# The second transform with 128 + 65 contraction rows for all four kinds

## The chip, the core and the metric

The kernel runs on one core of one Trainium2 chip. The metric is the device time of one launch in microseconds (us), all four batches included. A core has a matrix engine (PE, with its weight loads listed as PEld), three elementwise engines (DVE, ACT, POOL), and DMA queues; each engine takes its own instructions in a fixed order, and semaphores tie the engines together.

## The reference

There are 4 batches of 768 tokens with 8 heads of 48 channels (384 in all). What is computed, cut to what matters:

```python
for t in range(S):                       # complex linear recurrence with decay a (normalized)
    S_re, S_im = ar*S_re - ai*S_im + kv, ar*S_im + ai*S_re
    y[:, :, t] = einsum('bhd,bhde->bhe', q[:, :, t], S_re)
x = y                                    # as (batch, 768, 384)
u = x + real(fft(fft(x, axis=1), axis=2))
un = (u - mean) / sqrt(var + 1e-6)
v = u + relu(un @ w_ch1) @ w_ch2
u2 = v + token_mlp(v)                    # 768 -> 256 -> 768 over the tokens
out = u2 + relu(u2 @ w3) @ w4
```

## The kernel before

**Two streams.** A batch passes through a chain (`stage1`: the recurrence, a scan on DVE, ACT and POOL, then attention-like matmuls in chunks of 96 tokens; `stage2`: the two-axis transform and the normalization) and then through a dense stream (`mlp`, `tok1`, `tok2`: matmuls of 128 x 384 in three passes each, lines 989 and 1011 above all). The chain of batch b+1 is written next to the dense stream of batch b, so PE has dense matmuls to run while the chain waits. Batch 0 has no dense stream beside its chain: there, conversions of the weights (ACT, DVE, POOL) and warming matmuls (`warm`, L320) run in the gaps. After the chain of batch 3 only dense work is left.

**Order.** The source gives each instruction a priority by stream (`RANK`, `Prio`), and the order of every engine's queue is made when the program is built: a list scheduler walks a simulated timeline and gives an engine that comes free the ready instruction of best priority. On the chip each queue then runs in that fixed order. A tile framework adds the semaphores: it tracks which columns of a tile an instruction reads and writes.

**stage2.** All of its data lie in one 128 x 12288 tile, the one that holds the two halves K and Q of stage 1 (the trace calls it `qkt`). `WSP` (L1019) gives each part its columns; the folded columns `fd` lie at 3072 to 6160, over K of chunks 4 to 7, and K of chunk 7 is read last by the score matmuls of that chunk (L809).

1. `folds` (L1040) adds and subtracts the two halves of the 768 tokens (L1047, L1053), as the output of stage 1 (`xT`) comes in.
2. `mirrors` (L1059) folds columns n and 384 - n into `fd` (L1063; the unpaired columns 0 and 192 by ACT copies, L1070). There are four kinds `ty`: cosine or sine for odd or even sums. They fill 192, 192, 193 and 191 of the 193 columns: `kinds` (L1038), where a sine kind is shifted by one column.
3. `dft` (L1073), called with `kt` 1 and 0, transforms the channels: for each kind four matmuls (L1079) whose stationary operand is `fd[:, ty, r, dt, n0:n0+n]`, 112 rows by n columns, and whose moving operand is 97 columns of cosines or sines. `n` comes from `ZK` (L1021): 128 for `kt` 0; for `kt` 1 it is 64, 64, 65 and 63. ACT copies the n result rows to `Z` (L1081).
4. `smm` (L1101) transforms the tokens: for one kind, two matmuls (L1104) add up over 128 rows and then `ZK[ty][1]` rows; the stationary operand is `smat` (constants, zero behind the last row of each kind), the moving one 193 columns of `Z`. There are eight calls per batch, in three groups `i`: kinds 0, 1; then 0, 2, 1, 3; then 2, 3, with four small matmuls for one extra row (L1109) ahead of the last one of kind 3. After each group ACT copies the result (L1140), POOL adds and subtracts its halves (L1141, L1142), PE transposes `xT` (L1151), and DVE joins both into `u` (L1156); statistics and `un` follow (L1163 to L1185), and `transposed` (L969) hands `un` to the dense stream.

All matmuls here are in 32-bit floats, and the trace lists each as two weight loads and two matmul records.

Of the kernel before, what the change touches and what calls it, by code (L numbers as in the profile page):

```python
# [53 lines left out]
def attn_fft_mixer_kernel(ctx: ExitStack, tc: tile.TileContext, aL, xL, vL, wL, qN, kN, vN, arN, aiN,  # L54
# [18 lines left out]
    ve, se, ge = Prio(nc.vector, "v"), Prio(nc.scalar, "v"), Prio(nc.gpsimd, "v")  # L73
# [28 lines left out]
    def palloc(tag, shape):  # L102
        n = 1
        for s in shape[1:]:
            n *= s
        if tag == "s":
            turn3[0] += 1
            tag = ("ssc", "s", "sp")[lent[0]]
            tag = tag[turn3[0] % len(tag)]
        t = psum.tile([128, 512], F32, tag=tag, bufs=PSB[tag], name=tag)  # L110
        v = t[0:shape[0], 0:n]
        if len(shape) == 3:
            v = v.rearrange("p (a b) -> p a b", b=shape[2])
        return v
# [861 lines left out]
    def mlp(u, b, p0, th, tl, done):  # L976
        for qd in range(4):
# [40 lines left out]

    WSP = {"xd": (0, 3072), "fd": (3072, 3088), "xf": (6160, 3072), "Z": (6160, 1552), "xr": (7712, 1536),  # L1019
           "smat": (9248, 2048), "cb": (0, 1737), "cc": (1737, 1158), "un": (3072, 2304)}  # L1020
    ZK = ((128, 64), (128, 64), (128, 65), (128, 63))  # L1021

    def stage2(b, space):
        def part(name, pat=None, **kw):
            o, n = WSP[name]
            v = space[:, o:o + n]
            return v.rearrange(pat, **kw) if pat else v
# [7 lines left out]
        xd = [[xd[:, s, r] for r in range(2)] for s in range(2)]  # L1035
        fd = part("fd", "p (t r a b) -> p t r a b", t=4, r=2, a=2)[0:112]
        Z = part("Z", "p (a b) -> p a b", a=8)
        kinds = ((0, 0, ALU.subtract, 0, 191), (1, 0, ALU.add, 1, 192), (2, 1, ALU.add, 0, 192), (3, 1, ALU.subtract, 1, 191))  # L1038

        def folds(k, o, n):  # L1040
# [32 lines left out]
        def dft(kt):  # L1073
            for ty in range(4):
                n0, n = 128 * kt, ZK[ty][kt]
                ps = palloc("s", [128, 2, 97])
                for r in range(2):
                    for dt in range(2):
                        te.matmul(out=ps[0:n, r, :], lhsT=fd[:, ty, r, dt, n0:n0 + n], rhs=dcos[0:112, ty % 2, dt, r, :],  # L1079
                                  start=(dt == 0), stop=(dt == 1))  # L1080
                se.copy(out=Z[0:n, 2 * ty + kt, :].rearrange("p (i r) -> p r i", r=2), in_=ps[0:n])  # L1081

# [18 lines left out]
        def smm(o, ty, j0, first, last, extra=False):  # L1101
            for kt in range(2):
                kk = ZK[ty][kt]
                te.matmul(out=o, lhsT=smat[0:kk, ty, kt, j0:j0 + 128], rhs=Z[0:kk, 2 * ty + kt, 0:193],  # L1104
                          start=(first and kt == 0), stop=(last and kt == 1))
                if extra and kt == 0:
                    for k2 in range(2):
                        kk = ZK[2][k2]
                        te.matmul(out=o[0:1], lhsT=fk[0:kk, k2:k2 + 1], rhs=Z[0:kk, 4 + k2, 0:193], start=False, stop=False)  # L1109

# [159 lines left out]
    def chain(b):  # L1270
        return stage2(b, stage1(b))
# [29 lines left out]
    with tc.If(fv != 0):  # L1301
        with tc.For_i(0, B, 1) as b:
            fallback(b)
            u, norm = stage2(B, alloc("qk", [128, 12288], name="ws"))
            t = transposed(u, norm, "s")
            dense2(B, u, *dense1(B, u, *t), row=b)
# [111 lines left out]
```

## Time and profile before

| what | us |
|---|---|
| median of 3 runs | 1066.04 |
| lowest and highest run | 1060.92, 1067.02 |
| the profiled execution, its own time | 1067.39 |
| its span in the profile | 1065.6 |

The span runs from the first to the last instruction of the program; some 1.8 us of the execution's time lie around it. Busy times are of that one execution. The ends of matmul records are modelled, so what a matmul costs is read from the distance between starts. A weight load can run under the matmul before it, so an idle stretch ahead of a weight load is time in which the engine had not let it begin.

### The profile page before, as it was taken

The numbers are of one execution on the slowest core, as the hardware profiler recorded it, in microseconds if no ns is written. First come the engines' busy times: TensorE is split into PE (matmuls) and PEld (weight loads), VectorE is DVE, ScalarE is ACT, GpSimd is POOL, SyncE is SP. The second block draws the span as 40 slices with busy tenths as digits, with TensorE's granted clock in tenths as the row PEclk, the third lists the DMA queues.
The fourth block names the chain that finished last, engine by engine and source line by source line (L and its number), as shares of the span: only waits on it lengthen the run. The fifth ranks groups of instructions, "written<-read, shape, count | busy, mean of one in ns | idle before, by whom it ended". The sixth has DMA issues, their size and how long they took to land.

```text
span 1065.6 us, 21108 instructions
## 1 busy us (share of the span) xinstructions
PE 976.5 (92%) x7326; PEld 916.8 (86%) x7326; DVE 750.0 (70%) x2078; ACT 507.5 (48%) x1423; POOL 393.3 (37%) x544
## 2 busy tenths in 40 slices
PE   1459896999889989999999999999999999999997
PEld 0238775999889878999998899999889999999997
DVE  6986867999998696999768979984844433433332
ACT  6752546877775335678413766842233212111211
POOL 5632765555464782346336412424622002000000
PEclk9986987999999889999999999999999999999999
DMA  6226953678657942666575346655315434543522
GB/s 222 53 80 166 315 202 130 219 233 265 231 166 223 241 143 88 211 188 195 163 181 163 107 142 191 185 156 169 98 46 163 133 115 144 163 137 128 172 93 77
DMA packets 98337, 173.09 MB, mean 162 GB/s; under 512 B 10928, under 2 KB 57904, under 8 KB 97712
## 3 DMA queue, kind: packets, MB, share of 16 engines
q1 hardware_dynamic: 98224, 171.67, 52.4%
q8 instruction: 60, 0.98, 0.4%
q14 instruction: 53, 0.43, 0.1%
HBM read 132.31 MB, written 39.32 MB: 161 GB/s over the span
## 4 chain that ended last, share of the span: by engine, by line
PE 61%; DVE 2%; POOL 1%; DMA 1%; issue 1%; ACT 1%; SPq 0%; POOLq 0%; ACTq 0%
PE l L1011 22%; PE l L989 22%; PE s L809 2%; PE s L685 1%; PE s L1079 1%; PE s L1104 1%; PE s L1218 1%; PE s L1236 1%; DVE qkt L1053 1%; PE s L864 1%; PE c L1104 1%; PE c L685 1%; PE l L1236 1%; DMA cvt<-wL 1%; PE s L1151 1%
## 5 line engine op out<-in xcount | busy, mean ns | idle before, releaser
L1011 PE MATMUL l<-w,h 128*128 128x384 f32 x1728 | 325.8, 339 | 1.1 <-DVE h L1002 1.0
L989 PE MATMUL l<-th,w 128*128 128x384 f32 x1152 | 313.9, 341 | 4.1 <-ACT th L972 2.2
L1011 PEld LDWEIGHTS l<-w,h 128*128 128x128 f32 x1728 | 298.1, 188 | 4.5 <-DVE h L1002 2.1
L989 PEld LDWEIGHTS l<-th,w 128*128 128x128 f32 x1152 | 209.9, 189 | 6.4 <-ACT th L972 3.0
L993 ACT ACTIVATE h<-l 128x384 fp32r<-128x384 f32 x192 | 94.1, 491 | 211.4 <-PE l L989 211.1
L989 PE MATMUL l<-tl,w 128*128 128x384 f32 x576 | 194.3, 337 | 0.0
L1014 DVE TENSOR_TENSOR u<-u,l 128x384 f32<-128x384 f32 x192 | 105.4, 549 | 77.0 <-PE l L1011 75.9
L1002 DVE SCALAR_TENSOR_TENSOR h<-l,h 128x384 fp32r<-128x384 f32 x160 | 88.4, 553 | 88.7 <-ACT h L993 87.8
L989 PEld LDWEIGHTS l<-tl,w 128*128 128x128 f32 x576 | 108.9, 189 | 0.2
L207 POOL TENSOR_TENSOR cvt<-cvt 128x384 int32<-128x384 int32 x56 | 58.9, 1056 | 28.3 <-DVE cvt L205 22.9
L217 POOL TENSOR_TENSOR w<-cvt,w 128x384 fp32r<-128x384 f32 x44 | 46.0, 1050 | 52.2 <-ACT w L216 45.1
L1203 POOL TENSOR_TENSOR xl<-u,xh 128x384 fp32r<-128x384 f32 x18 | 18.1, 1015 | 98.0 <-ACT xh L1202 98.0
L499 PE MATMUL s<-misc,y 128*112 128x128 f32 x64 | 14.9, 378 | 42.1 <-DMA fk<-cFk 19.5
L203 ACT ACTIVATE cvt<-cvt 128x384 int32<-128x384 uint32 x56 | 31.3, 559 | 44.0 <-DMA cvt<-wL 41.2
L499 PEld LDWEIGHTS s<-misc,y 128*112 128x112 f32 x64 | 9.6, 181 | 47.9 <-POOL ss L463 22.8
L634 POOL TENSOR_TENSOR A<-raw,tm 128x144 f32<-128x144 f32 (+1 forms) x51 | 25.4, 499 | 61.9 <-DVE tm L632 24.7
L1000 POOL TENSOR_TENSOR h<-full,h 128x384 fp32r<-128x384 f32 x32 | 33.0, 1030 | 39.0 <-ACT full L999 37.2
L658 DVE TENSOR_TENSOR p<-p,A 128x144 f32<-128x144 f32 x144 | 44.6, 310 | 1.6
L616 POOL TENSOR_TENSOR tm<-tm 128x144 f32<-128x144 f32 (+1 forms) x51 | 25.3, 498 | 45.3 <-ACT tm L615 43.0
L660 DVE TENSOR_TENSOR p<-p,yt 128x96 f32<-128x96 f32 x144 | 37.5, 260 | 2.2
L809 PE MATMUL s<-qkt 112*96 112x96 f32 x328 | 38.6, 267 | 0.0
L845 POOL TENSOR_TENSOR yc<-Aa,gm 48x384 f32<-48x384 f32 x18 | 19.8, 1101 | 48.1 <-DVE Aa L835 47.7
(310 smaller groups left out, 2023.4 us busy)
## 6 DMA issues: line engine op xcount, KB each, us to landing
w<-wscr SPq DMA_DIRECT2D x180, 384.0 KB, 3.6
cvt<-wL SPq DMA_DIRECT2D x56, 384.0 KB, 4.6
wscr<-w SPq DMA_DIRECT2D x44, 384.0 KB, 3.0
Kn<-kn SPq DMA_DIRECT2D x56, 192.0 KB, 4.2
kn<-y SPq DMA_DIRECT2D x96, 96.0 KB, 2.6
raw<-aL SPq DMA_DIRECT2D x48, 144.0 KB, 3.4
xx<-xL SPq DMA_DIRECT2D x48, 144.0 KB, 3.3
V<-vL SPq DMA_DIRECT2D x32, 144.0 KB, 3.2
```

Source lines behind the costliest of these rows:

```text
L203: se.activation(out=lo, in_=lo.bitcast(U32), func=ACTF.Copy, scale=2.0 ** -29)
L207: x = ge.tensor_tensor(out=a, in0=a, in1=lo, op=ALU.add)
L217: ge.tensor_tensor(out=parts[:, 1, :], in0=a.bitcast(F32), in1=r32(parts[:, 0, :]), op=ALU.subtract)
L658: ve.tensor_tensor(out=cur, in0=prev, in1=A[:, j, 0:3, :], op=ALU.mult)
L660: ve.tensor_tensor(out=cur[:, 0:2, :], in0=cur[:, 0:2, :], in1=y, op=ALU.add)
L809: te.matmul(out=ps[:, j, :], lhsT=K[:, hc, :], rhs=Q[:, hc, :])
L989: te.matmul(out=ps, lhsT=w1[:, wi, kt * 128:kt * 128 + 128], rhs=x[g][:, kt, :], start=(n == 0), stop=(n == 8))
L993: x = se.activation(out=hi, in_=ps, func=ACTF.Relu)
L1000: ge.tensor_tensor(out=lo, in0=full, in1=r32(hi), op=ALU.subtract)
L1002: ve.scalar_tensor_tensor(out=lo, in0=ps, scalar=0.0, in1=r32(hi), op0=ALU.max, op1=ALU.subtract)
L1011: te.matmul(out=ps, lhsT=hs[m][:, hi, tt * 128:tt * 128 + 128], rhs=w2[:, wi, :], start=(n == 0), stop=(n == 8))
L1014: ve.tensor_tensor(out=u[tt], in0=u[tt], in1=ps, op=ALU.add)
```

## The change

The contraction of `kt` 1 gets 65 rows for every kind, where it had 64, 64, 65 and 63: `dft(1)` loads 65 columns of `fd` as weights and makes 65 rows of `Z`, and the second matmul of each `smm` contracts 65 rows. So that the added columns hold zeros, `stage2` first sets columns 191 and 192 of all 16 rows of `fd` to zero, by one DVE instruction per call; the mirrors and copies of the kinds that use those columns write them afterwards. `smat` needs no change. The number of matmuls, their moving columns and the DMAs stay as they are.

```diff
@@ -1018,7 +1018,7 @@
-    ZK = ((128, 64), (128, 64), (128, 65), (128, 63))
+    ZK = ((128, 65),) * 4
@@ -1035,6 +1035,7 @@
         fd = part("fd", "p (t r a b) -> p t r a b", t=4, r=2, a=2)[0:112]
         Z = part("Z", "p (a b) -> p a b", a=8)
+        ve.memset(fd[:, :, :, :, 191:193], 0.0)
         kinds = ((0, 0, ALU.subtract, 0, 191), (1, 0, ALU.add, 1, 192), (2, 1, ALU.add, 0, 192), (3, 1, ALU.subtract, 1, 191))
```

## Rows read from the trace of the kernel before

**Rows 1.** The page: the span, and PE's busy time, share and instructions.
```profile
span 1065.6 us, 21108 instructions
PE 976.5 (92%) x7326; PEld 916.8 (86%) x7326; DVE 750.0 (70%) x2078; ACT 507.5 (48%) x1423; POOL 393.3 (37%) x544
```

**Rows 2.** The page: the chain that ended last, shares of the span.
```profile
PE 61%; DVE 2%; POOL 1%; DMA 1%; issue 1%; ACT 1%; SPq 0%; POOLq 0%; ACTq 0%
```

**Rows 3.** Windows in stage 2: stretch, length, busy us of PE, PEld, DVE, ACT, POOL, clock.
```profile
155.70:166.50 10.80, 10.23 (x56) 6.95 (x55) 5.95 (x18) 4.33 (x11) 9.03 (x13) 1.00 0.37 146
...
389.50:395.20 5.70, 5.65 (x29) 5.25 (x29) 5.67 (x13) 3.00 (x12) 5.70 (x7) 0.50 0.18 51
...
579.00:609.00 30.00, 29.58 (x190) 25.52 (x189) 27.21 (x96) 19.76 (x65) 16.44 (x29) 1.00 0.51 155
764.00:792.00 28.00, 28.00 (x182) 24.05 (x181) 14.06 (x44) 11.16 (x28) 9.60 (x12) 1.00 0.22 71
```

**Rows 4.** Waits of PE between 575 and 800 us: total, times, longest.
```profile
PE s L864 <- issue: 1.3, 1, 1.3
...
PE c L1079 <- POOL qkt L1063: 0.4, 1, 0.4
```

**Rows 5.** Timeline of PE, batch 2: start us, duration us, group of records.
```profile
598.88 3.76 PE L1104 MATMUL c<-qkt 128*128 128x193 f32 x16
...
606.54 1.15 PE L1104 MATMUL c<-qkt 128*128 128x193 f32 x6
```

**Rows 6.** Timeline of PEld, the same stretch; in brackets the idle time before.
```profile
599.30 0.29 PEld L1104 LDWEIGHTS c<-qkt 64*128 64x128 f32 x2 [0.23 <-issue]
599.82 0.96 PEld L1104 LDWEIGHTS c<-qkt 128*128 128x128 f32 x6 [0.23 <-issue]
601.00 0.29 PEld L1104 LDWEIGHTS c<-qkt 64*128 64x128 f32 x2 [0.23 <-issue]
```

**Rows 7.** Groups of L1104 by shape, 580 to 615 us: count | busy, mean ns.
```profile
L1104 PE MATMUL c<-qkt 64*128 64x193 f32 x8 | 2.4, 375 | 0.0
...
L1104 PE MATMUL c<-qkt 65*128 65x193 f32 x4 | 1.0, 327 | 0.0
```

**Rows 8.** All of L1104: idle time of PEld before it, us, times.
```profile
  issue: 8.4, 35
```

**Rows 9.** Timeline of PE, batch 3: the channel transform.
```profile
764.86 0.88 PE L1079 MATMUL s<-dcos,qkt 112*64 112x97 f32 x8
765.58 0.83 PE L1079 MATMUL c<-dcos,qkt 112*64 112x97 f32 x8
766.34 0.88 PE L1079 MATMUL s<-dcos,qkt 112*65 112x97 f32 x8
```

**Rows 10.** Groups by shape, 760 to 800 us: weight loads of the channel transform.
```profile
L1079 PEld LDWEIGHTS s<-dcos,qkt 112*65 112x65 f32 x8 | 0.7, 136 | 0.1
...
L1079 PEld LDWEIGHTS s<-dcos,qkt 112*63 112x63 f32 x8 | 0.7, 135 | 0.2 <-ACT qkt L1081 0.2
```

**Rows 11.** Timeline of ACT, end of batch 0's stage 2.
```profile
165.82 0.48 ACT L1140 COPY qkt<-s 128x386 f32<-128x386 f32 x1 [2.10 <-PE s L1104]
166.20 0.21 ACT L1173 ACTIVATE rs<-rs 128x2 f32<-128x2 f32 x1
```

**Rows 12.** Timeline of PE, the same part: the first transposes to the dense stream.
```profile
171.20 1.11 PE L969 MATMUL s<-misc,qkt 128*128 128x128 f32 x4 [3.63 <-DVE qkt L1185]
```

**Rows 13.** Groups of DVE by shape: memsets of the kernel before.
```profile
L420 DVE MEMSET p<- 64x48 f32 x2 | 0.2, 98 | 0.8 <-PEq L1408 0.8
...
L128 DVE MEMSET ones<- 128x1 f32 x1 | 0.1, 59 | 0.0
```

**Rows 14.** Timeline of DVE, batch 2: the first fold.
```profile
567.72 0.96 DVE L1047 TENSOR_TENSOR qkt<-xT 112x768 f32<-112x768 f32 x1 [0.83 <-ACT xT L872]
```

**Rows 15.** Timeline of PE, batch 2: the scores of chunk 7.
```profile
569.04 0.84 PE L809 MATMUL s<-qkt 112*96 112x96 f32 x8
```

**Rows 16.** Timeline of PE, batch 1: the first group of the channel transform.
```profile
389.55 0.88 PE L1079 MATMUL p<-dcos,qkt 112*64 112x97 f32 x4 [2.19 <-DVE qkt L1063]
```

## The prediction

> **What bounds the kernel now.** I read the page first. PE is busy for 976.5 of 1065.6 us [rows 1], and the chain that ended last lies on PE for 61% of the span, on no other engine for more than 2% [rows 2]. So time taken from PE should count, if it is taken where PE has nothing to wait for. Next I read windows around the four calls of `stage2` [rows 3]. In batches 2 and 3 PE is full (29.58 of 30.00 us, 28.00 of 28.00), since dense matmuls fill what the transform leaves; between 575 and 800 us its longest wait is 1.3 us, and one wait of 0.4 us belongs to the transform [rows 4]. Batch 1 has one dry spell: PE waits 2.19 us for a mirror on DVE [rows 16], and then runs for 5.70 us at a granted clock of 0.50, the lower of its two levels (1.2 instead of 2.4 GHz) [rows 3]. In batch 0 nothing dense is at hand, and PE is busy for 10.23 of 10.80 us in the token transform [rows 3].
>
> Then I read the matmuls that change. A "busy" PE can hide a loss, so I read starts, not durations. In the timeline of weight loads an idle stretch of 0.23 us stands ahead of each load of 64 rows, and the same ahead of the first 128-row load behind it [rows 6]. The releaser is given as "issue": nothing that the profile knows was late. Inside the group of six loads at 599.82 (128, 65, then 128 rows of kinds 0, 2, 1) no idle time is listed: from 128 to 65 rows PE goes on. So it is the step between over 64 rows and at most 64 that costs. The means agree: a matmul record of 64 rows takes 375 ns, one of 65 rows 327 [rows 7]. Over the kernel these stops come 35 times ahead of L1104, 8.4 us of idle loader in all [rows 8]; the stops that follow a small matmul and stand ahead of another line come on top.
>
> **Part 1: the token transform.** Of the eight `smm` of a batch six end in 64 or 63 rows. The last of them comes behind the one-column matmuls of L1109, and the step from one weight column stays a step. So a batch loses 5 steps in and 6 out, 11; four batches lose 44. The price of one: 16 records without dense work between span 3.76 us and hold 5 steps [rows 5]. A record's own length at the end is 0.33 [rows 7], so 15 distances take 3.43. Six records with no step span 1.15, so 5 distances take 0.82, or 0.165 each [rows 5]. 15 x 0.165 is 2.48, the excess 0.95, and a step costs 0.19 us. It is less than the idle 0.23 because a load otherwise starts under the matmul before. All of PE: 44 x 0.19 = 8.4 us.
>
> Batches 1 to 3: 33 x 0.19 = 6.3 us, counted whole, because PE is full there. Batch 0: 11 x 0.19 = 2.1 us. There ACT waits 2.10 us for the last `smm` group, and a rescaling step, L1173, is queued right behind that copy [rows 11]; the norm of the first tokens needs it, and PE idles 3.63 us for the norm [rows 12]. So an earlier end of `smm` passes through ACT to the dense stream. DVE's chain behind it sets part of this end and may keep some: 0 to 2.1, I take 1.5.
>
> **Part 2: the channel transform.** It has the step in the number of weight columns. In batch 3 two groups of eight 64-column records start 0.72 us apart, while the 65-column group starts 0.76 behind the second [rows 9]. Counting from the second group's start to its end 0.83, the next starts 0.07 before that end; the second started 0.16 before the first one's (764.86 + 0.88). That is 0.09 lost at the step, and the group behind a step is 0.05 longer (0.88 against 0.83): 0.14 us each. In batches 1 to 3 I count nine such steps that stand beside no longer wait: two or three a batch where dense work or another kind comes between, 1.3 us; those beside a wait, and batch 0's, I count at nothing (upper end: six more, 0.8). The added column costs nothing that can be seen: a load of 65 columns takes 136 ns, one of 63 takes 135 [rows 10]. The ACT copies of 65 rows have as many columns as those of 63.
>
> **Part 3: the memset.** It writes 32 elements in 112 rows. The nearest rows are 59 ns for 1 element and 98 for 48 [rows 13]; I take 0.09 us, 0.4 in all. It lies on DVE, which in batches 1 to 3 is not what PE waits for but at the dry spell; I count it at 0 (upper end 0.4). Its wait matters more. `fd` lies over K of chunk 7, so the memset waits for the scores of chunk 7, which the mirrors did before; but in the source it stands ahead of the folds. If it is also queued ahead of them, folds and the dense stream's DVE work behind it wait. In batch 2 the first fold starts at 567.72 [rows 14], the scores end at 569.04 + 0.84 = 569.88 [rows 15]: at most 2.2 us of DVE, before mirrors that start later anyway. POOL's and ACT's writes to `fd` already wait for DVE's folds, so they gain no later wait. I take 0 because the list scheduler gives the queue to what is ready first; the upper end is 4 x 2.2 = 8.8.
>
> **Sum.** 6.3 + 1.5 + 1.3 = 9.1 us. Against the profiled execution: 1067.4 - 9.1 = 1058.3. That execution lies 1.35 us above the median, so from the median it is 1056.9. I forecast 1057.5, between them. All steps at full price and no cost give 8.4 + 2.1 = 10.5, which is 1056.9 or, from the median, 1055.5.
>
> **Rivals.**
> 1. *The memset stalls the folds* in each batch (8.8 us): 1067.4 - 9.1 + 8.8 = 1067, no change. For it: its place in the source. Against: folds and memset have one stream's priority, and only the ready one is taken.
> 2. *PE runs dry ahead of the channel transform in more batches*, the other side. The queues are ordered anew when the program is built, with one more DVE instruction per batch; where the folds come behind more dense additions on DVE, PE has no matmul left. For it: it happens in batch 1. Against: nothing in the change asks for it. Price from batch 1: 2.19 us idle, and half of 5.70 us at the lower clock, 2.85: 5.0 each. From two more spells on, it eats the gain; three give 1067.4 - 9.1 + 15.0 = 1073.3.
> 3. *The new order takes batch 1's dry spell away*: 1058.3 - 5.0 = 1053.3. Nothing speaks for it but that the queues are made anew.
> 4. *PE's time is not what counts*: the steps go, and PE waits as much longer for the chain. Then batch 0's 1.5 us are left: 1066. Against it stand the full windows [rows 3].
> 5. *It does not do what it says*: a 65-row load stops PE as well. The group at 599.82 speaks against it [rows 6]. Then the time stays at 1067. The Trainium skill ("TensorE: Matmul & The Clock Gate", Part 3, the mechanism) has a rule that would lead there: weight loads overlap running matmuls only where their row groups differ, and 65 rows share theirs with the 128 before. By that rule the gain is nothing and the time 1067; the trace disagrees, for the loads at 599.82 run on without idle time.
>
> **How the numbers follow.** Forecast 0.58 (its own range 1054.5 to 1061, from the bounds of parts 1 to 3 and the two baselines); rivals 1 to 5: 0.10, 0.09, 0.10, 0.08, 0.05. The range 1052 to 1067 holds the forecast, rivals 3 and 4 and about half of rivals 1 and 5. About 1% is what a measurement of this kernel can tell from no change: 10.7 us, just over the most that the steps can give. Faster by over 1% is rival 3 and a part of the forecast's lower end: 0.25. Slower by over 1% is the worse half of rival 2: 0.05. Within 1%: 0.70.
>
> **What would show it.** Right: no idle stretch of 0.23 us ahead of L1104 but at the one-column matmuls; means of 327 ns for all its records; 16 records in some 2.8 us; PE still full in batches 1 to 3. Wrong: those stops stay (5); the stops go and PE's waits in stage 2 grow (2, 4); a memset with idle time before it on DVE, and folds behind it (1). A gain far over 10 us would mean that the order changed elsewhere.

## The result, and the profile after

The changed kernel took 1053.98 us (median of 6 runs, 1052.39 to 1054.83) beside 1063.09 for the kernel before (6 runs, 1058.87 to 1067.02): a ratio of 0.9916, 95% interval 0.9892 to 0.9941, or 9 us. Two later sets of runs of the same kernel gave 0.9910 and 0.9931.

The page of the changed kernel, its span and busy times (against [rows 1]):

```profile
span 1052.9 us, 21114 instructions
PE 962.4 (91%) x7326; PEld 914.9 (87%) x7326; DVE 752.1 (71%) x2082; ACT 507.2 (48%) x1423; POOL 391.1 (37%) x544
```

PE's busy time falls by 14.1 us with the same number of instructions, the weight loader's by 1.9. Not all of the 14.1 is the change: a second profile of the kernel before, taken below, has 970.7 us, 5.8 less than the first. The four more DVE instructions are the memsets. One line was added, so lines behind 1038 are one higher than in the kernel before.

The token transform of batch 2 on PE, 584 to 599 us (against [rows 5]); columns as there:

```profile
584.37 1.57 PE L1105 MATMUL c<-qkt 128*128 128x193 f32 x8
...
589.37 2.79 PE L1105 MATMUL c<-qkt 128*128 128x193 f32 x16
...
595.91 1.15 PE L1105 MATMUL c<-qkt 128*128 128x193 f32 x6
```

The same on the weight loader (against [rows 6]):

```profile
584.36 1.28 PEld L1105 LDWEIGHTS c<-qkt 128*128 128x128 f32 x8
...
589.20 2.66 PEld L1105 LDWEIGHTS c<-qkt 128*128 128x128 f32 x16
...
595.74 1.02 PEld L1105 LDWEIGHTS c<-qkt 128*128 128x128 f32 x6
596.99 0.41 PEld L1110 LDWEIGHTS c<-qkt,fk 128*1 128x1 f32 x4 [0.23 <-issue]
...
597.73 0.30 PEld L1105 LDWEIGHTS c<-qkt 65*128 65x128 f32 x2 [0.33 <-issue]
```

Sixteen records now span 2.79 us, not 3.76, while the six that never had a step still span 1.15. The loader goes through a whole group in one row, without a bracket; what is left stands at the one-column matmuls. Over the kernel, idle time of the loader ahead of this line (against [rows 8]) is

```profile
  issue: 1.3, 4
```

where it was 8.4 us in 35 stops. The groups by shape, 570 to 605 us (against [rows 7]), and the windows of the transform in batches 2 and 3 (against [rows 3]):

```profile
L1105 PE MATMUL c<-qkt 65*128 65x193 f32 x16 | 4.0, 333 | 0.0
```
```profile
570.00:600.00 30.00, 29.40 (x205) 28.10 (x204) 27.49 (x97) 20.47 (x67) 16.91 (x30) 1.00 0.51 159
754.00:782.00 28.00, 28.00 (x198) 26.98 (x198) 15.34 (x50) 12.79 (x31) 9.43 (x14) 1.00 0.25 77
```

The mean of 333 ns is that of 16 records, of which one, behind the one-column matmuls, takes 431 and the others some 327. PE is about as full as before (29.40 of 30 us and 28.00 of 28, where it was 29.58 and 28.00), and within 28 us it starts 198 records where it started 182.

### The profile page after: what moved, and what is told of

Read it like the earlier page. It is cut to its first block, busy times and chain, and to the rows that moved or that the text cites. A ratio compares the mean times of both kernels' runs of the same rounds, so it can differ in the third digit from the quotient of the medians.

```text
span 1052.9 us, 21114 instructions
## 1 busy us (share of the span) xinstructions
PE 962.4 (91%) x7326; PEld 914.9 (87%) x7326; DVE 752.1 (71%) x2082; ACT 507.2 (48%) x1423; POOL 391.1 (37%) x544
## 4 chain that ended last, share of the span: by engine, by line
PE 57%; DVE 4%; POOL 2%; ACT 2%; issue 1%; DMA 1%; POOLq 0%
PE l L1011 21%; PE l L989 21%; PE s L809 1%; PE s L685 1%; PE s L1219 1%; PE s L1237 1%; PE s L1105 1%; PE s L1080 1%; PE s L864 1%; POOL cvt L207 1%; PE c L685 1%; PE l L1237 1%; DVE qkt L1054 1%; PE s L969 1%; PE c L809 1%
```

## The experiments

To compare profiles I read, for each batch, two lengths between record starts from PE's timeline: first to last record of the token transform ("token"), and first record of the channel transform to first of the token transform ("channel"). One table, in us; batch 0 last because its clock differs:

| kernel | token, batches 1, 2, 3 | channel, batches 1, 2, 3 | batch 0: token, channel | span |
|---|---|---|---|---|
| before, 1st profile | 11.8, 15.5, 15.5 | 12.3, 13.6, 11.0 | 9.7, 20.6 | 1065.6 |
| before, 2nd | 11.8, 15.5, 15.5 | 11.2, 13.6, 11.0 | 9.7, 15.5 | 1060.6 |
| before, 3rd | 11.8, 15.5, 15.5 | 11.2, 13.6, 11.0 | 9.7, 21.0 | 1064.4 |
| memset alone | 11.8, 15.5, 15.5 | 11.2, 13.5, 11.0 | 9.7, 15.5 | 1058.5 |
| channel transform alone | 11.8, 15.5, 15.5 | 10.7, 13.6, 10.6 | 9.7, 18.6 | 1061.3 |
| token transform alone | 9.9, 13.6, 13.6 | 11.2, 13.6, 11.0 | 7.9, 17.1 | 1054.3 |
| changed, 1st | 9.9, 13.6, 13.6 | 10.8, 13.6, 10.6 | 7.8, 15.6 | 1052.9 |
| changed, 2nd | 9.9, 13.6, 13.6 | 12.0, 13.6, 10.6 | 7.9, 15.2 | 1050.9 |
| changed, 3rd | 9.9, 13.6, 13.6 | 11.7, 13.6, 10.6 | 7.8, 14.8 | 1052.7 |
| changed, no memset | 9.9, 13.6, 13.6 | 10.7, 13.6, 10.5 | 7.8, 15.2 | 1051.9 |
| kind 2 with 64 rows | 12.6, 16.2, 16.2 | 12.4, 13.6, 11.0 | 10.5, 17.1 | 1063.4 |
| regrouped | 10.5, 14.6, 14.5 | 14.3, 13.3, 11.7 | 8.8, 17.1 | 1055.9 |
| 128 columns, 1st | 9.6, 13.3, 13.3 | 10.8, 13.6, 10.6 | 7.6, 18.7 | 1056.5 |
| 128 columns, 2nd | 9.6, 13.3, 13.3 | 10.8, 13.6, 10.6 | 7.6, 18.0 | 1053.3 |

Three explanations stood against each other: the steps (the forecast, "step theory"); a clock in batch 0 that the change keeps up, since there the first two profiles differ most ("clock theory"); and a new order of the queues ("order theory"). For the third the two profiles at hand already leave little room: DVE, ACT and POOL start the same instructions in the same order in both kernels, but for the four memsets on DVE.

**The changed kernel again.**

> The changed kernel once more, for a second profile. Between the two profiles at hand the channel transform of batch 0 took 20.6 us before and 15.6 after, because PE's granted clock was 0.54 for 10.5 us of it before and 1.00 after. Step theory: the gain is the steps (33 x 0.19 + 9 x 0.14 = 7.6 us in batches 1 to 3, up to 1.9 in batch 0's token transform), and the clock in batch 0 falls in some executions of either kernel: ratio near 0.9915, and the clock in batch 0 may be low here. Clock theory: some 5 of the 9 us are the clock of batch 0, which the change keeps up: it is at 1.00 here as well.

0.9910, interval 0.9879 to 0.9940. Batch 0's clock was high again. That did not part the theories, since the high clock could still be the change's doing; the kernel before had to be looked at again, below.

**The token transform alone.**

```diff
-    ZK = ((128, 64), (128, 64), (128, 65), (128, 63))
+    ZK = ((128, 64), (128, 64), (128, 65), (128, 63)); ZS = ((128, 65),) * 4
...  in smm:
-                kk = ZK[ty][kt]
+                kk = ZS[ty][kt]
```

> Only the token transform contracts 65 rows for all kinds; the channel transform keeps 64, 64, 65, 63, and there is no memset (the rows behind the end meet zeros of the constants). The order of every queue is that of before, instruction by instruction. Step theory: 44 steps of 0.19 us go, 6.3 us in batches 1 to 3 and 0.4 to 1.9 in batch 0: 6.7 to 8.2 us faster, ratio 0.992 to 0.994. Clock theory: the channel transform of batch 0 is as before, so its low clock stays in the profile, and the gain is about 4 us, ratio 0.996. Order theory (a new order made the gain): no change.

0.9932, interval 0.9910 to 0.9954: by the ratio 7.2 us faster, within step theory's 6.7 to 8.2, with no instruction in another place. Its timeline has the rows of the changed kernel (584 to 600 us, PE):

```profile
590.32 2.79 PE L1104 MATMUL c<-qkt 128*128 128x193 f32 x16
...
596.86 1.15 PE L1104 MATMUL c<-qkt 128*128 128x193 f32 x6
```

The token stretch is 1.9 us shorter in each of the four batches. Ten of the eleven steps of a batch lie within it: 0.19 each. This run settles it, by its stretches more than by its whole time: order theory gave no change here and falls, but clock theory gave 4 us, and 3 us is what whole times of one kernel differed by in this series (below). That the stretches shrink by the price of the steps in all four batches, with batches 1 to 3 at a granted clock of 1.00 there, is what no clock in batch 0 explains.

**The channel transform alone**, with the memset: the change, but `smm` reads the old row counts.

```diff
-    ZK = ((128, 65),) * 4
+    ZK = ((128, 65),) * 4; ZS = ((128, 64), (128, 64), (128, 65), (128, 63))
...  in smm:
-                kk = ZK[ty][kt]
+                kk = ZS[ty][kt]
```

> Memset and 65 columns in the channel transform as in the change; the token transform contracts 64, 64, 65 and 63 rows as before. Every queue has the order of the changed kernel. Step theory: nine steps of 0.14 us go, 1.3 us faster, ratio 0.999. Clock theory: the clock of batch 0 stays at 1.00, 5 to 6 us faster, ratio 0.995. Order theory: nearly the whole gain, ratio 0.992.

0.9996, interval 0.9973 to 1.0018. This has the changed kernel's order in every queue and next to none of its gain, so order theory falls here too. Batch 0 had a low clock for a part of the stretch in spite of the 65 columns (18.6 us). Of the forecast 1.3 us the stretches show 0.5 in batch 1 (11.2 to 10.7, both with a clock of 0.72 over the first 6 us), nothing in batch 2 and 0.4 in batch 3. Why nothing in batch 2: the groups themselves are shorter, but what they gain is lost ahead of two of them. PE's timeline around 576 us, here and in the second profile of before:

```profile
575.85 1.50 PE L1080 MATMUL s<-dcos,qkt 112*65 112x97 f32 x16
...
577.90 0.88 PE L1080 MATMUL c<-dcos,qkt 112*65 112x97 f32 x8 [0.54 <-POOL qkt L1064]
```
```profile
574.64 1.55 PE L1079 MATMUL s<-dcos,qkt 112*64 112x97 f32 x16
...
576.62 0.88 PE L1079 MATMUL c<-dcos,qkt 112*65 112x97 f32 x8 [0.43 <-POOL qkt L1063]
```

Sixteen records end 0.05 us sooner, and the wait for POOL's mirror is 0.11 longer. The later groups win some 0.3 us more, and all of it goes ahead of the last group of 128 columns. Its loads, and the end of ACT's queue before them, here and in the second profile of before:

```profile
587.15 0.34 ACT L1082 COPY qkt<-s 65x194 f32<-65x194 f32 x1
587.60 1.86 PEld L1080 LDWEIGHTS s<-dcos,qkt 112*128 112x128 f32 x16 [0.35 <-issue]
```
```profile
585.88 0.33 ACT L1081 COPY qkt<-s 63x194 f32<-63x194 f32 x1
586.33 1.89 PEld L1079 LDWEIGHTS s<-dcos,qkt 112*128 112x128 f32 x16
```

In both kernels these loads begin 0.11 to 0.12 us behind the end of ACT's copy of the group of kind 3; before without idle time, now with 0.35 us of it. That the copy is what they wait for is not shown: the profile names no releaser.

**The change without its memset.**

```diff
-        ve.memset(fd[:, :, :, :, 191:193], 0.0)
```

> The change without the memset: 65 columns and rows everywhere, what lies behind the folded columns meets zeros of the constants. Step theory with a free memset: ratio 0.9915 as the change. If the memset or the order that it brings costs something, this is faster than the change by up to 0.4 us (its own time) or by the stall that it makes; if the new order helps, it is slower.

0.9908, interval 0.9877 to 0.9940, beside 0.9910 for the changed kernel in the same set: the memset costs nothing that can be told.

**The kernel before, twice more.**

> The kernel before once more, for a second profile and as the measure of no change: ratio 1.000. The stretch from the first channel-transform matmul of batch 0 to the first of the token transform took 20.6 us in the first profile of before, 15.1 to 15.5 in two of the changed kernel and one without the memset, but 17.1 with the token transform alone changed and 18.6 with the channel transform alone. If the low clock there comes and goes by itself in any kernel, it may be short here (15 to 18 us); if the old 64-column channel transform brings it about, it is near 20 again.

1.0029, interval 1.0012 to 1.0047, in a kernel that is the same: some 3 us is what a whole time in this series can be off by, more than its interval says. The second profile has batch 0's clock at 1.00, the third (set below) at 0.53. Windows, first of the second profile, then of the third; the clock is the third number from the end:

```profile
140.00:146.00 6.00, 6.00 (x44) 5.07 (x43) 4.76 (x13) 4.16 (x11) 2.38 (x3) 1.00 0.58 195
```
```profile
137.50:148.00 10.50, 10.20 (x40) 8.32 (x41) 5.89 (x17) 3.79 (x9) 2.35 (x3) 0.53 0.42 128
```

> The kernel before a third time: ratio 1.000, where the second gave 1.003, so it bounds what a ratio in this series can tell. A third look at batch 0's channel transform, which took 20.6 us at a clock of 0.54 in one profile of this kernel and 15.5 at 1.00 in the other.

1.0005, interval 0.9984 to 1.0027. So the low level (1.2 GHz) in batch 0's channel transform comes and goes in one and the same kernel, and the 5 us that it makes of the 12.7 between the first two profiles come and go without the change.

**The memset alone.**

```diff
-        Z = part("Z", "p (a b) -> p a b", a=8)
+        Z = part("Z", "p (a b) -> p a b", a=8); ve.memset(fd[:, :, :, :, 191:193], 0.0)
```

> The kernel before with the memset alone: contractions of 64, 64, 65 and 63 rows, the queues in nearly the order of the changed kernel. Step theory: the same time as before, ratio 1.000, at most 0.4 us slower by the memset's own time. Order theory: a part of the gain, ratio below 0.997. Stall of the folds: slower by up to 8.8 us, ratio 1.008.

1.0005, interval 0.9984 to 1.0026. No stall, and no gain from the order.

**More steps.** Kind 2 too gets 64 rows in the token transform, so the kernel leaves out the last row of that kind.

```diff
-    ZK = ((128, 64), (128, 64), (128, 65), (128, 63))
+    ZK = ((128, 64), (128, 64), (128, 65), (128, 63)); ZS = ((128, 64), (128, 64), (128, 64), (128, 63))
...  in smm:
-                kk = ZK[ty][kt]
+                kk = ZS[ty][kt]
```

> The kernel before, but the token transform contracts 64 rows for kind 2 too, so it leaves out that kind's last row. Every queue has the order of before. Kind 2 then steps in and out twice per batch more (in the second group between kinds 0 and 1, in the third ahead of kind 3 and behind the first matmul): 4 steps per batch more, 16 in all. Step theory: 12 x 0.19 = 2.3 us slower in batches 1 to 3 and up to 0.8 in batch 0, ratio 1.002 to 1.003; idle stretches of 0.23 us ahead of the token transform rise from 35 by about 16. Rival (PE's time is taken up elsewhere): no change in time though the idle stretches rise.

1.0047, interval 1.0030 to 1.0064. The unchanged kernel beside it read 1.0029, so the whole time alone does not show that the steps make it slower, or by how much. The loader's idle time ahead of this line shows the steps:

```profile
  issue: 12.0, 51
```

Sixteen stops more, as counted, and 0.7 to 0.8 us more in each token stretch for four steps: 0.19 each.

**The same matmuls in another order.** This parts "a step costs" from "a 64-row matmul is slow". In each group of the token transform all 128-row matmuls come first, then those of 64 and 63 rows, then that of 65 (`smm` gets an argument `kts` that names the parts to run):

```diff
...  group i == 1 of three (the others alike):
-                    smm(ps[:, pq, :], pq, 128, True, False)
-                    smm(ps[:, pq, :], 2 + pq, 128, False, True)
+                    [smm(ps[:, x % 2, :], x, 128, x == 0, x == 2, kts=(kt,)) for kt, xs in ((0, (0, 1, 2, 3)), (1, (0, 1, 3, 2))) for x in xs if pq]
```

> The kernel before with its 64, 64, 65 and 63 rows, but the matmuls of a token-transform group in another order: all of 128 rows first, then those of 64 and 63, then the one of 65. Same matmuls, 5 steps per batch instead of 11. The queues are made anew, so the whole time can move by some us either way; the token-transform stretches tell. Step theory: 35 idle stretches of the loader ahead of this line fall to under 20, and the stretch of batches 2 and 3 falls from 15.8 to 15.9 us by 6 x 0.19 = 1.1. Rival (a 64-row matmul is slow by itself): the records of 64 rows keep a mean of 375 ns and the stretches stay.

0.9977, interval 0.9957 to 0.9998. Groups by shape, 560 to 620 us:

```profile
L1104 PE MATMUL c<-qkt 64*128 64x193 f32 x8 | 1.8, 349 | 0.0
...
L1104 PE MATMUL c<-qkt 65*128 65x193 f32 x4 | 1.2, 380 | 0.0
...
L1104 PE MATMUL c<-qkt 63*128 63x193 f32 x4 | 1.1, 350 | 0.0
```

Now the 65-row matmuls are the slow ones (380 ns, 327 before [rows 7]), because each comes behind one of 63 rows, and those of 64 rows fall from 375 to 349, since only one in two follows a 128-row matmul. Slowness goes with the step. The loader's stops fall from 35 to 20, where under 20 was expected, and the token stretches by 0.9 to 1.3 us, where 1.1 was. The queues were made anew here and the channel stretch of batch 1 grew to 14.3, so the whole time gained less than the stretches.

**The last steps.** In the changed kernel the small matmuls for the extra row get 128 weight columns, 127 of them zeros.

```diff
-            "smat": (9248, 2048), ...
+            "smat": (9248, 2304), ...
-                        te.matmul(out=o[0:1], lhsT=fk[0:kk, k2:k2 + 1], ...
+                        te.matmul(out=o, lhsT=sall[0:kk, 2048 + 128 * k2:2176 + 128 * k2], ...
```

> The changed kernel, and the four small matmuls for the extra row get 128 weight columns (one that counts and 127 of zeros, kept behind the other constants, whose DMA grows by an eighth) instead of 1. That takes the last two steps of each batch: 8 in all, 6 of them in batches 1 to 3. Step theory: 1.1 to 1.5 us faster than the changed kernel, ratio to before 0.9895 where the changed kernel has 0.991. Rival: weight loads of 128 columns instead of 1 (0.19 us instead of 0.08) lie bare on PE and eat the gain: no faster than the changed kernel.

0.9936, interval 0.9914 to 0.9958: no faster than the changed kernel had been in the other sets. Its profile had batch 0's low clock for a part of the stretch, so it was run again, beside the changed kernel, whose engines have nearly the same order.

> The changed kernel a third time, beside the next kernel and one more look at batch 0's clock. Ratio to before 0.991. If the low clock of batch 0's channel transform comes and goes by itself, it may be here; so far it is in 1 of 4 profiles of kernels with the whole change (that with 128 columns for the extra row), and in 4 of 6 of the kernels with a part of it or none.

0.9931, interval 0.9907 to 0.9955, clock of batch 0 high.

> The kernel with 128 weight columns for the extra row again: its engines have the order of the changed kernel, its token transforms were 0.3 us shorter in each batch in the first profile (8 steps fewer), and its time was no better. Step theory: about 1 us faster than the changed kernel beside it, ratio 0.990. Rival (the larger constants' DMA, or the clock, takes it back): the same or slower.

0.9909, interval 0.9881 to 0.9936; medians 1054.43 against 1055.65 for the changed kernel beside it. The weight loader, 580 to 600 us:

```profile
596.13 1.02 PEld L1105 LDWEIGHTS c<-qkt 128*128 128x128 f32 x6
597.12 0.68 PEld L1110 LDWEIGHTS c<-qkt 128*128 128x128 f32 x4
597.78 0.35 PEld L1105 LDWEIGHTS c<-qkt 65*128 65x128 f32 x2
```

No stop is left ahead of these lines, and each token stretch is 0.3 us shorter in both profiles. That is 1.1 us in all, which the whole times cannot tell from nothing: they are of opposite sign, and in the first set the changed kernel did not run beside it. It is not shown to beat the changed kernel.

## Why the prediction was right, point by point

**What bounds the kernel.** Right where it counted. In batches 1 to 3 the token stretches lost 1.9 us each, and the same steps taken alone made the kernel 7.2 us faster. The waits of PE that [rows 4] shows stayed within 0.2 us, but between 565 and 790 us one has come up that the kernel before has not, the last of these:

```profile
PE s L864 <- issue: 1.1, 1, 1.1
...
PE c L1080 <- POOL qkt L1064: 0.5, 1, 0.5
PE s L969 <- DVE u L1157: 0.4, 1, 0.4
```

It stands in batch 2, ahead of the transposes that hand the result to the dense stream, and it is in all profiles of kernels with the whole change and in that of the token transform alone, but in none of the others: PE now comes to these transposes before DVE's `u` is there. So 0.4 us of the 6.3 that the prediction counted whole came back as a wait. In both profiles with 128 weight columns it is 0.7: what the last steps give in that batch, 0.3 us, PE waits longer.

**Part 1.** The price of a step (0.19 us), the count (44), and 16 records in 2.8 us came out as worked out. Taking PE's starts instead of its busy share made the difference: the busy share counted the stops as work [rows 3]. One slip has no effect: the six loads at 599.82 [rows 6] are of kinds 2, 2 and 1, not 0, 2 and 1. The Trainium skill has a rule that fits, in "TensorEngine Tiling (Array Packing)", Key Properties: changing the tiling mode, not only the tile, drains the engine. The regrouped run agrees with it in that the stop stands at the change and not at the small matmul; that the steps here are changes of that mode is not shown, for no record of the trace names a mode. For batch 0, 1.9 us went in the token stretch, as bounded. How much of it reached the end is not settled: from the last token matmul of batch 0 to the first channel matmul of batch 1 the changed kernel took 224.5 to 227.7 us in three profiles, the kernel before 224.1 to 225.0. With the token transform alone it took 224.7, so there most of the 1.9 us arrived at batch 1, in the one profile taken. The 1.5 us that I took is neither shown nor refuted.

**Part 2.** The mechanism was right, the size not. The term of 1.3 us measured about 0.9 in the stretches (0.5, 0.0, 0.4), and the whole time of that part alone could not tell 0.4 us from nothing. The step that failed is the count: I took nine steps as standing beside no longer wait; in batch 2 the waits for POOL's mirror (0.11 us longer) and ahead of the last group (0.35 us of idle loader, none before) took back what the groups gained.

**Part 3.** Right. The memset took 85 ns and was queued behind folds, not ahead of them. In batch 2 of the changed kernel (DVE's timeline; against [rows 14]):

```profile
564.21 1.37 DVE L1054 TENSOR_TENSOR qkt<-qkt 112x384 f32<-112x384 f32 x1
...
565.55 0.09 DVE L1038 MEMSET qkt<- 112x32 f32 x1
...
566.46 0.54 DVE L816 TENSOR_TENSOR sc<-c,misc 96x384 f32<-96x384 f32 x1
```

The scores of chunk 7 had ended by 561.2 us, so it had no idle time before it. Alone it made no difference in time. One small trace of it is there: PE's wait ahead of batch 1's channel transform is 2.41 us in the profiles of the memset alone, the channel transform alone and the changed kernel, and 2.19 to 2.20 in those of the kernel before, the token transform alone and the change without its memset.

**The rivals.** Rival 1 falls with that row. Rivals 2 and 3 did not come, nor did the new order on which they rest: batch 1's dry spell stayed (2.4 us for `xT` in the first profile of the changed kernel, 2.19 before [rows 16]) and batches 2 and 3 have none; its lower clock varies the channel stretch of batch 1 from 10.7 to 12.4 us in kernels of either kind. Rival 4 falls with the token transform alone, but for the wait of 0.4 us above. Rival 5 falls with the unbroken loader rows, and with it what the Trainium skill's rule on row groups ("TensorE: Matmul & The Clock Gate", Part 3, the mechanism) would have given: loads of 128 and 65 rows, which share theirs, follow one another without idle time (16 in 2.66 us).

**The number.** The sum of 9.1 us stands beside 9 in the first set, 9.6 and 7.3 in the later ones. That it comes so close is in part luck: batch 0's 1.5 us was picked from a range, part 2 gave 0.9 for 1.3, 0.4 us came back as a wait, and whole times can be off by some 3 us. Nor is batch 0's clock wholly out of the 9 us, since it differed between profiles; spans of profiles in which its channel transform had the upper level throughout are 1060.6 us for the kernel before and 1058.5 with the memset alone, against 1050.9 to 1052.9 for the changed kernel, 5.6 to 9.7 us less. What carries the sum is part 1: 33 x 0.19 = 6.3 us in three batches, and batch 0. The absolute time, 1053.98, fell under the forecast 1057.5 and just under the forecast's own range (1054.5 to 1061), because I started from a profiled execution and a median that lay above what the kernel before took over six and more runs (1063.09). It came to stand next to rival 3's 1053.3; the dry spell that stayed rules that cause out.

## To carry to other kernels

Read the starts of matmuls and the idle time ahead of weight loads, not PE's busy share: a stop that the releaser calls "issue", and that comes back with one length (0.23 us here) at the same change of shape, is a cost of the instructions' shapes. Where matmuls of 64 or 63 contraction rows or weight columns alternate with larger ones, as here, zeros that make them 65 take the stops away, and an order that groups them takes some; that pays in full only where PE is the engine that has work waiting. Take one more profile of the unchanged kernel before a stretch that differs between two profiles is put down to a change.

## What the runs showed of the hardware that was not expected

PE's clock in batch 0's channel transform stood at its upper level for the whole stretch in some executions and near the lower one for up to 10 us in others, of one program: 15.5 us in one profile of the kernel before, 20.6 and 21.0 in two. Ahead of that part PE was idle for about 2 us in nearly 5, in every case, mostly for DVE's mirrors: 2.2 and 2.8 us in the profiles of before with the low clock, 1.8 in the one without, 2.1 in the first of the changed kernel, which kept the high clock. The token transform alone idled for 1.9 us, less than that, and fell to the lower level all the same, for a short part:

```profile
138.80:141.00 2.20, 2.20 (x7) 1.56 (x6) 1.67 (x7) 1.75 (x3) 0.00 (x0) 0.50 0.99 270
```

So that idle time alone does not decide it. The four profiles of the changed kernel, with and without its memset, all had the upper level there, both of the kernel with 128 columns the lower one for a part. Whether the change makes the low stretch rarer stays open: the runs of the kernel before are spread over some 10 us (1057.86 to 1068.44), those of the changed one over 4 (1052.39 to 1056.55), but those of the kernels with one part of the change are spread over 7 to 8 (12 runs each), and no run took the wait ahead of the stretch away.
